# Linear attention and two gated feed-forward layers on one core: the norm's factor of tile 0 put on sums, slice groups of 3, 4 and 5, low parts by way of DRAM, decays on VectorE

## The chip, the core and the metric

The kernel runs on one core of a Trainium2 chip. A core has TensorE (matmuls out of SBUF into eight PSUM banks), VectorE, ScalarE and GpSimd for elementwise work, and queues from which DMA transfers are issued; SP's queue (SyncE) issues most of them here. The metric is the device time of one execution in microseconds. Three runs of the kernel before took 655.06, 658.07 and 658.17 us.

## What is computed

Three stages follow each other: causal linear attention with a decay for each head (in blocks of 64 in the reference, whose result doesn't depend on the block), an RMS norm with a gated layer (silu), and a second gated layer without silu.

```python
# attention, B=2, H=8, S=768, D=64, for each block of positions
intra = einsum('bhic,bhjc->bhij', qb, kb) * Dmask          # lam ** (i-j), i >= j
out[block] = einsum('bhij,bhjd->bhid', intra, vb) + einsum('bhid,bhde->bhie', qb * lam_pow, kv_state)
kv_state = lam_block * kv_state + einsum('bhsd,bhse->bhde', kb * rev_pow, vb)
...
# x: (1536, 512) tokens; first layer, d_ff = 1536
rms = sqrt(mean(x * x, axis=-1) + 1e-6);  xn = x / rms * rms_g
g = xn @ w_gate;  x = (g / (1 + exp(-g)) * (xn @ w_val)) @ w_out
# second layer
out = ((x @ w_a) * (x @ w_b)) @ w_out2
```

## The kernel before

**Tiles and slices.** The 1536 tokens are three tiles of 512 (`TILES`): tile 0 holds chunks 0 and 1 of 128 positions for both batch rows, tile 1 chunks 2 and 3, tile 2 chunks 4 and 5. The 1536 hidden features of a layer are 12 slices of 128; slices 0 to 11 are those of the first layer, 12 to 23 those of the second.

**High and low parts.** Every feed-forward product is made of three matmuls on halves: high weight with high input, high with low, low with high. ScalarE rounds a high part (`unit_hi`, word `hi` or `uh`), VectorE subtracts it from the original to get the low part (`unit_lo`, `lo` or `ul`). Both live in pools of six buffers each. Weights come in as 64-bit numbers and are first put together as 32-bit ones: two copies on ScalarE (`c`) and six operations on VectorE (`k`), for a slice's three parts together, or by pieces of 512 columns.

**Direct steps and pairs.** A direct step is one slice on one tile: a gate run G and a value run V of 12 matmuls each (`proj`), silu (`si`), product (`mu`), the two halves of it (`hh`, `hl`) and an output run O of 12 matmuls that adds into the four banks `acc0` to `acc3`. The other slices take tiles 1 and 2 together as a 2x2 block product with seven products instead of eight (`product`, word P, six matmuls each), with sums of weight blocks (`ws`) and of results (`ps`, `pa`) ahead and behind; their output runs are Q. `GROUPS` sets which slices share an accumulation: the first group of the first layer is direct on all three tiles, later groups and the whole second layer are direct on tile 0 alone and pairs on tiles 1 and 2. At a group's end `E` (or `e`) copies or adds the banks into the tile's sums (`tile_sum`).

**Attention** of a batch row b and chunk c is a handful of short TensorE groups: S (scores), X (within the chunk), I (from the state), U (state update), R (mean of squares by a column of ones) and N (the token factors, spread over the partitions by a matmul with a diagonal). VectorE masks the scores (`am`); GpSimd multiplies the keys and queries by their decays (`kd`, `qd`), decays the state (`sd`) and takes the power -1/2 (`rr`). The norm then multiplies x by g and the factor (`nx`) and splits it into tile halves (`xh`, `xl`). For chunks 2 on, VectorE first adds up the squares over the four column blocks (`rd`), so that R is one matmul and not four. W are matmuls on zeros that only keep TensorE busy.

**Order.** Nothing is scheduled: `PROGRAM` is a list of words written out by hand, run from first to last; each word issues its instructions, and each engine and each DMA queue works off its own in that order. A word `G.3` is the gate run of step 3, `X.1.0` the X of b=1, c=0, `l.6` the load of a weight part on SP's queue.

Of the kernel before, what the change touches and what calls it, by code (L numbers as in the profile page):

```python
# [38 lines left out]
GROUPS = [(0, 6), (6, 12)]  # L39

SLOTS, OUT_SLOTS = 7, 10


LAST_ATT = 11
# [4 lines left out]
    A.0.0.0 W.8.1 W.14 W.3.1 W.7.1 W.2.1 S.0.0 W.3.1 A.0.0.2 l.0 g Z A.1.0.0 A.1.0.2 D.0 D.1 A.0.1.0 A.1.1.3  # L49
    A.1.1.0 l.1 l.2 A.0.1.2 A.1.1.2 c.0.1 S.1.0 l.3 A.0.1.3 k.0.0.1 k.0.1.1 k.0.3.1 k.0.4.1 k.0.5.1 k.0.2.1  # L50
    am.0.0.0 am.0.0.1 am.1.0.0 am.1.0.1 k.0.6.1 X.0.0 kd.1.0 U.1.0 X.1.0 sq.0.0 xg.1.0 kd.0.0 S.0.1 U.0.0 hi.0.0
    xg.0.0 sa.1.0 sa.0.0 R.0.0 ms.0.0 am.0.1.0 am.0.1.1 lo.0.0 L.0.2 sq.1.0 c.0.2 S.1.1 R.1.0 k.0.0.2 am.1.1.1
    k.0.1.2 ms.1.0 c.1.0 qd.0.1 I.0.1 k.0.4.2 am.1.1.0 k.0.3.2 k.0.5.2 k.0.2.2 qd.1.1 kd.1.1 X.0.1 I.1.1 W.3.1
    sd.0.1 rr.0 dg.0 N.0 kd.0.1 W.3.1 U.1.1 W.3.1 X.1.1 U.0.1 xg.0.1 c.1.1 k.0.6.2 hi.0.1 nx.0.1 nx.0.0 xh.0.0
    sq.0.1 nx.0.2 nx.0.3 xh.0.1 xg.1.1 l.4 l.10 l.5 R.0.1 sd.1.1 lo.0.1 xl.0.0 sa.1.1 sa.0.1 ms.0.1 xl.0.1 sq.1.1
    R.1.1 ms.1.1 c.1.2 k.1.0 L.1.2 k.1.1 c.2.0 qd.0.2 kd.0.2 rr.1 dg.1 k.1.4 k.1.3 N.1 nx.1.3 nx.1.2 nx.1.0 nx.1.1
# [812 lines left out]
```

## Time and profile before

| | |
|---|---|
| three runs | 655.06, 658.07, 658.17 us (median 658.07) |
| profiled execution | 655.5 us, its span 653.8 us |
| TensorE busy | 638.9 us, 98% |
| VectorE busy | 520.1 us, 80% |
| ScalarE busy | 405.0 us, 62% |
| GpSimd busy | 39.7 us, 6% |

The span runs from the first to the last instruction of the profiled execution; 1.7 us lie around it. Busy times of engines overlap each other. A TensorE group's own duration includes its pipeline's drain, so consecutive groups overlap by a little.

### The profile page before, as it was taken

The page shows a single profiled execution, that of the slowest core. Times are in us where ns is not written, and L with a number is a line of the kernel's source. Part 1 is how long each engine was busy: PE and PEld are TensorE (multiplying, and loading weights), DVE is VectorE, ACT ScalarE, POOL GpSimd, SP SyncE. Part 2 cuts the span into 40 slices and gives each one's busy share as a digit, 9 for nine tenths or more (in the row PEclk, how much of TensorE's full clock was granted, in tenths as well). Part 3 has the DMA queues.
Part 4 walks back from the last instruction along what each step waited for, and adds up shares of the span by engine and source line. Part 5 has one row for each costly group of instructions (what it writes and reads, how often), then busy time and mean ns, then how long its engine had stood idle before and what let it go on. Part 6 is the DMA issues. An engine that isn't in the chain of part 4 may idle for free.

```text
span 653.8 us, 8719 instructions
## 1 busy us (share of the span) xinstructions
PE 638.9 (98%) x3304; PEld 517.5 (79%) x3306; DVE 520.1 (80%) x889; ACT 405.0 (62%) x642; POOL 39.7 (6%) x43
## 2 busy tenths in 40 slices
PE   9989999999999999999999999999999999999997
PEld 4767777787888888878887888888887888888876
DVE  4789999655579999889999988857968688776664
ACT  2878853332599884379888655665559873444441
POOL 1533122110000000000000000000000000000000
PEclk9969999999999999999999999999999999999999
DMA  8945641110036520013233120020023220100011
GB/s 262 378 156 188 226 161 65 65 65 1 4 127 194 162 96 1 1 36 126 66 99 127 64 65 1 0 66 33 1 96 97 67 63 1 65 1 0 2 64 65
DMA packets 16506, 54.84 MB, mean 84 GB/s; under 512 B 1864, under 2 KB 3408, under 8 KB 15440
## 3 DMA queue, kind: packets, MB, share of 16 engines
q1 hardware_dynamic: 15600, 47.99, 22.2%
q10 hardware_dynamic: 864, 6.29, 2.7%
q8 instruction: 26, 0.43, 0.3%
q14 instruction: 16, 0.13, 0.1%
HBM read 51.12 MB, written 3.15 MB: 83 GB/s over the span
## 4 chain that ended last, share of the span: by engine, by line
PE 86%; DVE 9%; DMA 2%; SPq 1%; ACT 1%; issue 0%; POOL 0%; ACTq 0%; DVEq 0%; POOLq 0%
PE acc L562 27%; PE at L706 15%; PE gv L706 11%; PE gv L514 6%; PE gv L518 6%; PE gv L515 5%; PE at L515 3%; PE at L514 3%; PE at L518 3%; DMA att<-att_dram 1%; DVE sums L574 1%; PE at L393 1%; PE at L358 1%; DVE wlo L317 1%; PE at L408 1%; DVE hh L301 1%
## 5 line engine op out<-in xcount | busy, mean ns | idle before, releaser
L260 ACT COPY hh<-stage 128x1024 uint8<-128x1024 uint8 x72 | 75.2, 1045 | 6.7 <-DMA stage<-w_dram 6.5
L514 PE MATMUL gv<-xhi,whi 128*128 128x512 f32 x192 | 76.7, 399 | 0.0
L317 DVE TENSOR_TENSOR wlo<-w,whi 128x512 fp32r<-128x512 f32 (+1 forms) x108 | 69.7, 654 | 7.8 <-ACT whi L312 7.8
L515 PE MATMUL gv<-xlo,whi 128*128 128x512 f32 x192 | 74.9, 390 | 0.0
L312 ACT CAST whi<-w 128x512 fp32r<-128x512 f32 (+1 forms) x108 | 60.5, 585 | 14.1 <-PE acc L562 5.6
L537 ACT CAST hhi<-s 128x512 fp32r<-128x512 f32 x36 | 22.4, 622 | 50.7 <-DVE s L533 49.1
L317 DVE TENSOR_TENSOR wlo<-o,whi 128x512 fp32r<-128x512 f32 x72 | 50.5, 705 | 3.5 <-ACT whi L312 3.4
L518 PE MATMUL gv<-xhi,wlo 128*128 128x512 f32 x192 | 51.6, 391 | 1.4 <-DVE wlo L317 1.4
L264 ACT COPY w<-stage 128x1024 uint16<-128x1024 uint16 x48 | 50.2, 1045 | 0.0
L312 ACT CAST whi<-o 128x512 fp32r<-128x512 f32 x72 | 44.2, 620 | 8.9 <-PE acc L562 4.3
L518 PEld LDWEIGHTS gv<-xhi,wlo 128*128 128x128 f32 x192 | 35.9, 188 | 9.7 <-DVE wlo L317 2.2
L562 PE MATMUL acc<-hlo,whi 128*128 128x512 f32 x144 | 42.1, 392 | 0.9 <-DVE hlo L541 0.6
L562 PE MATMUL acc<-whi,hlo 128*128 128x512 f32 x144 | 42.9, 391 | 0.0
L514 PEld LDWEIGHTS gv<-xhi,whi 128*128 128x128 f32 x192 | 36.1, 188 | 8.4 <-issue 0.9
L562 PE MATMUL acc<-hhi,whi 128*128 128x512 f32 x144 | 42.5, 395 | 0.2
L562 PE MATMUL acc<-whi,hhi 128*128 128x512 f32 x144 | 42.2, 392 | 0.1
L562 PE MATMUL acc<-wlo,hhi 128*128 128x512 f32 x144 | 41.8, 390 | 0.0
L515 PEld LDWEIGHTS gv<-xlo,whi 128*128 128x128 f32 x192 | 36.1, 188 | 7.0
L562 PE MATMUL acc<-hhi,wlo 128*128 128x512 f32 x144 | 41.5, 390 | 0.0
L706 PE MATMUL at<-T,whi 128*128 128x512 f32 x144 | 38.5, 389 | 0.0
L514 PE MATMUL at<-xhi,whi 128*128 128x512 f32 x96 | 37.3, 389 | 0.0
L515 PE MATMUL at<-xlo,whi 128*128 128x512 f32 x96 | 37.3, 389 | 0.0
(167 smaller groups left out, 1405.0 us busy)
## 6 DMA issues: line engine op xcount, KB each, us to landing
stage<-w_dram SPq DMA_DIRECT2D x72, 512.0 KB, 3.4
att<-att_dram ACTq DMA_DIRECT2D x6, 1024.0 KB, 4.8
att<-att_dram SPq DMA_DIRECT2D x6, 512.0 KB, 5.6
out_dram<-sums SPq DMA_DIRECT2D x12, 256.0 KB, 2.1
att<-att_dram SPq DMA_DIRECT2D x2, 1024.0 KB, 8.3
att<-att_dram SPq DMA_DIRECT2D x4, 256.0 KB, 9.6
dt<-ext_d SPq DMA_DIRECT2D x2, 256.0 KB, 4.7
p<-ext_d SPq DMA_DIRECT2D x2, 128.0 KB, 4.6
```

Of the source, the lines that this page charges most:

```text
L260: nc.scalar.copy(hh_t[i][:, into].bitcast(U8).rearrange("p (n e) -> p n e", e=2), st.rearrange("p (n e) -> p n e", e=8)[:, :, 3:5],)
L264: nc.scalar.copy(home(i, slice(place, place + 1)).bitcast(U16).rearrange("p (n e) -> p n e", e=2), st.bitcast(U16).rearrange("p (n e) -> p ...
L301: nc.vector.tensor_tensor(out=hh, in0=hh, in1=t, op=ALU.bitwise_or)
L312: nc.scalar.copy(whi[key], src)
L317: nc.vector.tensor_sub(wlo[key], src, whi[key].bitcast(F32))
L358: nc.tensor.matmul(ps[r][:, a * C : (a + 1) * C], lhsT=t[r * D : (r + 1) * D, 1, a * C : (a + 1) * C], rhs=t[r * D : (r + 1) * D, 0, a * C ...
L514: nc.tensor.matmul(ps, lhsT=w, rhs=xhi[t][:, k, :], start=k == 0, stop=False)
L515: nc.tensor.matmul(ps, lhsT=w, rhs=xlo[t][:, k, :], start=False, stop=False)
L518: nc.tensor.matmul(ps, lhsT=w, rhs=xhi[t][:, k, :], start=False, stop=k == KD - 1)
L537: nc.scalar.copy(h_t[g][0], s_t[g])
L562: nc.tensor.matmul(acc[j], lhsT=lhsT, rhs=rhs, start=first and n == 0, stop=last and n == 2)
L706: nc.tensor.matmul(ps, lhsT=w[:, k * 128 : (k + 1) * 128], rhs=x[:, k, :], start=first and n == 0, stop=n == len(todo) - 1, skip_group_che ...
```

## The change

Four things change together, and with them the written-out order.

- **Norm of tile 0.** Chunks 0 and 1 go from their bank straight to tile 0's high and low halves with g alone (`xs`, `xd`). The token factors are kept in `rv`; `gs` multiplies the gate's sums by them ahead of silu, and after the last group `sr` multiplies the first layer's sums of tile 0, since the value half and the output product are linear in them. Chunks 2 to 5 are normed as before.
- **Groups.** The first layer has groups of 3, 4 and 5 slices, so 3 slices are direct on all tiles and 9 are pairs on tiles 1 and 2; the second keeps 6 and 6.
- **Low parts by way of DRAM.** The low parts of slices 0 to 2, made for tile 0, are stored (`ls`) and read back for tiles 1 and 2 (`lr`), in SP's queue: 9 stores, 18 loads of 256 KB. The high parts are rounded again.
- **Decays.** Keys and queries are multiplied on VectorE, from chunk 2 on mostly both in one instruction of 1024 columns (`qk`); the state decay moves there too. GpSimd copies the key decays once into a table (`dk`) and keeps the power. R of chunks 2 and 3 is four matmuls, as that of chunks 0 and 1; `rd` stays for chunks 4 and 5. Nine of the 46 W matmuls go, eight output buffers stay of ten.

```diff
-GROUPS = [(0, 6), (6, 12)]
...
+GROUPS = [[(0, 3), (3, 7), (7, 12)], [(0, 6), (6, 12)]]
...
+def beside(i, t):
+    return i < GROUPS[0][0][1] and t < 2 or i < GROUPS[0][1][1] and t == 0
...
-LAST_ATT = 11
...
-    A.0.0.0 W.8.1 W.14 W.3.1 W.7.1 W.2.1 S.0.0 W.3.1 A.0.0.2 l.0 g Z A.1.0.0 A.1.0.2 D.0 D.1 A.0.1.0 A.1.1.3
...
+    W.3.1 W.2.1 W.7.1 A.0.0.0 W.8.1 S.0.0 W.3.1 W.14 A.0.1.2 g l.0 A.0.0.2 Z A.1.0.0 A.1.0.2 D.0 A.0.1.0 l.1 D.1
...
+    wlo_d = dpool.tile([GROUPS[0][0][1] * 3, 128, 512], F32, tag="wlo_d", name="wlo_d")
+
+    def lo_store(g, part):
+        nc.sync.dma_start(out=wlo_d[g * 3 + part], in_=wlo[g, part].bitcast(F32))
+
+    def lo_load(g, part):
+        wlo[g, part] = spool.tile([128, 512], F32R, tag="wlo", name="wlo")
+        nc.sync.dma_start(out=wlo[g, part].bitcast(F32), in_=wlo_d[steps[g][0] * 3 + part])
...
-    def key_decay(b, c):
...
-        nc.gpsimd.tensor_tensor(
-            out=kd_t[b, c],
...
-    def query_decay(b, c):
...
+    def decay(b, c, some):
+
+        if (b, c) not in kq_t:
+            kq_t[b, c] = kq if b == 0 else spare[:, 0:1024].rearrange("p (n j) -> p n j", n=2)
+        nc.vector.tensor_tensor(
+            out=kq_t[b, c][:, some], in0=att_t[b, c][:, 0:4:3][:, some], in1=kq_dec[:, some], op=ALU.mult
+        )
+
+    def decay_table():
+
+        nc.gpsimd.tensor_copy(
+            kq_dec[:, 1].rearrange("p (a r d) -> p a r d", a=NP, r=2),
+            dt[:, :, :, C - 1 : C].rearrange("p r a o -> p a r o").to_broadcast([128, NP, 2, D]),
...
     def state_decay(b, c):
-        nc.gpsimd.tensor_tensor(
+        nc.vector.tensor_tensor(
             out=st_t[b], in0=st_t[b], in1=p1[:, :, C - 1 : C].to_broadcast([128, NP, D]), op=ALU.mult
...
+    def att_hi(b, c):
+
+        hi = xtiles(0)[0]
+        for k in range(KD):
+            nc.scalar.mul(hi[:, k, c * 256 + b * C : c * 256 + (b + 1) * C], px_t[b, c][:, k * C : (k + 1) * C], g_sb[:, k, :])
+
+    def att_lo(b, c):
+        hi, lo = xtiles(0)
+        for k in range(KD):
+            some = (slice(None), k, slice(c * 256 + b * C, c * 256 + (b + 1) * C))
+            nc.vector.scalar_tensor_tensor(
+                out=lo[some], in0=px_t[b, c][:, k * C : (k + 1) * C], scalar=g_sb[:, k, :], in1=hi[some].bitcast(F32),
+                op0=ALU.mult, op1=ALU.subtract,
+            )
...
+    def factors(c):
+        nc.scalar.copy(rv[:, c * 256 : (c + 1) * 256], pr_t[c][:, 0:256])
...
-        for m in range(2) for lo, hi in GROUPS for t in range(1 if m or lo else len(TILES)) for f in range(lo, hi)
+        for m in range(2) for lo, hi in GROUPS[m] for t in range(1 if m or lo else len(TILES)) for f in range(lo, hi)
...
+    def gate_factors(g):
+        s_t[g] = hpool.tile([128, 512], F32, tag="s", name="s")
+        nc.vector.tensor_tensor(out=s_t[g], in0=pg_t[g], in1=rv, op=ALU.mult)
...
+        i, t, _, _ = steps[g]
+        if i < NF and t == 0:
+            nc.scalar.activation(s_t[g], s_t[g], AF.Silu)
+        else:
+            s_t[g] = hpool.tile([128, 512], F32, tag="s", name="s")
+            nc.scalar.activation(s_t[g], pg_t[g], AF.Silu if i < NF else AF.Copy)
...
+    def sum_factors(j):
+        nc.vector.tensor_tensor(out=sums[0][:, j, :], in0=sums[0][:, j, :], in1=rv, op=ALU.mult)
...
```

TensorE's queue ahead of the first gate run (rows with `xhi,whi` are gate matmuls; L454 is R, L478 N, L378 U, L358 S, L393 I, L408 X; the number behind `att_2` and the like only tells buffers apart). Before:

```order
L408 MATMUL acc_348<-am,att_1_186 64x128 x8
L378 MATMUL acc_396<-att_1_184,kd 64x64 x8
L454 MATMUL acc_429<-ones,sq 128x1 x4
L454 MATMUL acc_445<-ones,sq 128x1 x4
L478 MATMUL at_472<-nrm,ones 128x128 x2
L358 MATMUL at_486<-att_2_293 128x128
...
L378 MATMUL at_509<-att_2_293,kd 64x64 x8
L393 MATMUL at_518<-qd,st 64x128 x8
L408 MATMUL at_518<-am,att_2_293 64x128 x8
L514 MATMUL gv_535<-xhi_414,whi 128x512
```

The same place after the change (L489 is R, L513 N, L398 U, L378 S, L413 I, L428 X, L552 and L553 gate or value):

```order
L428 MATMUL acc_380<-am,att_1_192 64x128 x8
L489 MATMUL acc_399<-ones,sq 128x1 x4
L398 MATMUL acc_412<-att_1_175,kq 64x64 x8
L513 MATMUL at_421<-nrm,ones 128x128 x2
L378 MATMUL at_455<-att_2_435 128x128
...
L489 MATMUL acc_465<-ones,sq 128x1 x4
L552 MATMUL gv_494<-xhi_242,whi 128x512
...
L398 MATMUL at_507<-att_2_435,kq 64x64 x8
L513 MATMUL at_516<-nrm,ones 128x128 x2
L413 MATMUL at_522<-kq,st 64x128 x8
L428 MATMUL at_522<-am,att_2_435 64x128 x8
L552 MATMUL gv_576<-xhi_242,whi 128x512
```

U, N, I and X (the last three rows and the one ahead of them) stood ahead of the first gate run and now stand behind it, and between X and the scores of chunk 2 there is one R, one U and one N.

TensorE's queue at N of chunk 3, before (L514 and L515 are the gate run of step 5, or behind N the value run):

```order
L454 MATMUL at_1103<-ones,nrm 128x1
L514 MATMUL gv_1124<-xhi_414,whi 128x512
L515 MATMUL gv_1124<-xlo_415,whi 128x512
...
L518 MATMUL gv_1124<-xhi_414,wlo 128x512 x4
L478 MATMUL at_1137<-nrm,ones 128x128 x2
L514 MATMUL gv_1145<-xhi_414,whi 128x512
```

And after (L608 is the output run of step 1):

```order
L552 MATMUL gv_910<-xhi_242,whi 128x512
...
L556 MATMUL gv_910<-xhi_242,wlo 128x512 x4
L489 MATMUL at_931<-ones,sq 128x1 x4
L513 MATMUL at_942<-nrm,ones 128x128 x2
L608 MATMUL acc_796<-hhi,whi 128x512
```

Before, a gate run lies between the last R of chunk 3 and its N; now nothing does.

GpSimd's queue for chunk 1 to 2 before (L337 keys, L349 queries, L418 state, L468 the power):

```order
L468 TENSOR_TENSOR rr<-ms,mhalf 128x2
L337 TENSOR_TENSOR kd<-att_1_184,dt 128x512
L418 TENSOR_TENSOR st<-st,p_88 128x256
L349 TENSOR_TENSOR qd<-att_2_293,p_88 128x512
L337 TENSOR_TENSOR kd<-att_2_293,dt 128x512
```

VectorE's queue at the same chunks after (L362 decays, L438 the state decay, L309 and L315 pieces of a weight's conversion, L468 `xd`, L496 epsilon):

```order
L362 TENSOR_TENSOR kq<-att_1_175,dec 128x512
L309 TENSOR_SCALAR t<-hh 128x512
...
L438 TENSOR_TENSOR st<-st,dec 128x256 x2
L468 SCALAR_TENSOR_TENSOR xlo_243<-acc_380,g_sb,xhi_242 128x128 x4
L496 TENSOR_SCALAR ms<-acc_399 128x1
L362 TENSOR_TENSOR kq<-att_2_435,dec 128x1024
```

Products that GpSimd made by itself now stand among VectorE's conversions and remainders.

## Rows read from the trace of the kernel before

**Rows 1.** the page, part 1: busy us, share of the span, instructions.

```profile
PE 638.9 (98%) x3304; PEld 517.5 (79%) x3306; DVE 520.1 (80%) x889; ACT 405.0 (62%) x642; POOL 39.7 (6%) x43
```

**Rows 2.** the page, part 4: the chain that ended last, by engine.

```profile
PE 86%; DVE 9%; DMA 2%; SPq 1%; ACT 1%; issue 0%; POOL 0%; ACTq 0%; DVEq 0%; POOLq 0%
```

**Rows 3.** busy time by stretch (columns as in its second line).

```profile
core 0: us, PE busy (x) PEld busy (x) DVE busy (x) ACT busy (x) POOL busy (x), PEclk, DMA share, GB/s
...
44.40:111.80 67.40, 63.74 (x431) 50.50 (x429) 64.27 (x106) 47.31 (x69) 16.10 (x14) 1.00 0.47 160
...
165.00:285.00 120.00, 120.00 (x534) 99.45 (x533) 102.97 (x166) 85.80 (x133) 1.00 (x1) 1.00 0.25 80
```

**Rows 4.** the chain in order of time: start us, us, what.

```profile
108.05 2.72 PE acc L562 x12
```

**Rows 5.** TensorE in order of time: start us, us, what [idle before].

```profile
14.56 1.09 PE L408 MATMUL acc<-am,att 128*64 128x128 f32 x16
15.48 0.64 PE L378 MATMUL acc<-att,spare 128*64 128x64 f32 x16
...
17.02 1.16 PE L358 MATMUL at<-att 64*128 64x128 f32 x16
...
21.82 1.09 PE L393 MATMUL acc<-qd,st 64*64 64x128 f32 x16
...
30.10 1.05 PE L454 MATMUL acc<-ones,sq 128*128 128x1 f32 x8
...
34.62 1.22 PE L478 MATMUL at<-nrm,ones 128*128 128x128 f32 x4 [1.67 <-DVE nrm L473]
...
44.40 0.50 PE L514 MATMUL gv<-xhi,whi 128*128 128x512 f32 x1
...
47.27 0.28 PE L454 MATMUL at<-ones,nrm 128*128 128x1 f32 x2
```

**Rows 6.** busy time by stretch at the start, with the granted clock (PEclk).

```profile
24.00:33.00 9.00, 8.15 (x99) 6.03 (x96) 8.24 (x19) 8.08 (x13) 5.53 (x5) 1.00 0.91 348
...
36.00:44.00 8.00, 6.40 (x60) 5.43 (x62) 7.10 (x13) 5.19 (x6) 3.67 (x3) 0.52 0.55 179
```

**Rows 7.** GpSimd in order of time.

```profile
13.31 1.06 POOL L337 TENSOR_TENSOR spare<-att,dt 128x512 f32<-128x512 f32 x1 [10.88 <-DMA dt<-ext_d]
...
52.41 1.60 POOL L349 TENSOR_TENSOR qd<-att,p 128x512 f32<-128x512 f32 x1 [7.38 <-DMA att<-att_dram]
...
102.52 1.16 POOL L337 TENSOR_TENSOR spare<-att,dt 128x512 f32<-128x512 f32 x1 [0.74 <-DMA att<-att_dram]
```

**Rows 8.** VectorE in order of time.

```profile
52.78 1.77 DVE L317 TENSOR_TENSOR wlo<-o,whi 128x512 fp32r<-128x512 f32 x1
...
104.16 2.04 DVE L301 TENSOR_TENSOR hh<-hh,t 128x1536 uint16<-128x1536 uint16 x1
```

**Rows 9.** TensorE's waits, 44.4 to 135 us: us in total, times, longest.

```profile
PE at L378 <- DVE am L369: 1.6, 2, 1.1
PE gv L518 <- DVE wlo L317: 1.4, 2, 1.2
```

**Rows 10.** VectorE's groups, forms apart: count, busy us, mean ns, idle before.

```profile
L317 DVE TENSOR_TENSOR wlo<-w,whi 128x512 fp32r<-128x512 f32 x90 | 62.1, 701 | 7.8 <-ACT whi L312 7.8
...
L428 DVE TENSOR_TENSOR st<-st,at 128x256 f32<-128x256 f32 x6 | 2.5, 414 | 0.8 <-POOL st L418 0.5 <-PE at L378 0.3
...
L301 DVE TENSOR_TENSOR hh<-hh,t 128x512 uint16<-128x512 uint16 x3 | 1.3, 425 | 0.1
...
L665 DVE TENSOR_TENSOR sums<-sums 128x1024 f32<-128x1024 f32 x1 | 1.2, 1221 | 0.0
```

**Rows 11.** DMA issues: count, KB each, median us to landing.

```profile
out_dram<-sums SPq DMA_DIRECT2D x12, 256.0 KB, 2.1
...
att<-att_dram SPq DMA_DIRECT2D x4, 256.0 KB, 9.6
```

More of the change, by code (lines that the diff above doesn't have):

```diff
@@ L199, in chain_kernel @@
     dt = cpool.tile([128, 2, NP, C], F32, tag="dt", name="dt")
-    p1 = cpool.tile([128, NP, C], F32, tag="p1", name="p1")
+    kq_dec = cpool.tile([128, 2, 512], F32, tag="dec", name="dec")
+    p1 = kq_dec[:, 0].rearrange("p (a i) -> p a i", a=NP)
+    kq = tpool.tile([128, 2, 512], F32, tag="kq", name="kq")
     g_sb = cpool.tile([128, KD, 1], F32, tag="g_sb", name="g_sb")
+    rv = cpool.tile([128, 512], F32, tag="rv", name="rv")
     ones = cpool.tile([128, 128], F32, tag="ones", name="ones")
@@ L520, in gate @@
     def gate(g):
-        pg_t[g] = bank("at0" if g > LAST_ATT and g % 2 else "gv0")
+        pg_t[g] = bank("at0" if g % 2 and not beside(*steps[g][:2]) else "gv0")
         proj(pg_t[g], g, 0)
     def value(g):
-        pv_t[g] = bank("at1" if g > LAST_ATT and g % 2 else "gv1")
+        pv_t[g] = bank("at1" if g % 2 and not beside(*steps[g][:2]) else "gv1")
         proj(pv_t[g], g, 1)
+    def gate_factors(g):
+        s_t[g] = hpool.tile([128, 512], F32, tag="s", name="s")
+        nc.vector.tensor_tensor(out=s_t[g], in0=pg_t[g], in1=rv, op=ALU.mult)
     def silu(g):
-        s_t[g] = hpool.tile([128, 512], F32, tag="s", name="s")
-        nc.scalar.activation(s_t[g], pg_t[g], AF.Silu if steps[g][0] < NF else AF.Copy)
+        i, t, _, _ = steps[g]
[4 more added lines that the diff above has]
+            nc.scalar.activation(s_t[g], pg_t[g], AF.Silu if i < NF else AF.Copy)
     def gated(g):
@@ L567, in tile_sum @@
     def tile_sum(i, t, j):
-        if i % NF == GROUPS[0][1] - 1:
+        if i % NF == GROUPS[i // NF][0][1] - 1:
             if (t, i // NF) not in sums:
@@ L716, in snapshot @@
         elif n == 6:
-            pool, tag = H2_HOMES[i % 6]
-            s_t[i, 2] = pool.tile([128, 512], F32, tag=tag, name="h2")
+            pool, tag, half = H2_HOMES[i % 6]
+            if tag not in h2_t:
+                h2_t[tag] = pool.tile([128, 1024 if tag in ("kq", "dec") else 512], F32, tag=tag, name="h2")
+            s_t[i, 2] = h2_t[tag][:, half * 512 : half * 512 + 512]
             nc.scalar.copy(s_t[i, 2], px[i])
@@ L744, in pair_out @@
         f = i % NF
-        first, last = f in [x for x, _ in GROUPS], f + 1 in [x for _, x in GROUPS]
+        first, last = (f + n in [x[n] for x in GROUPS[i // NF]] for n in range(2))
         out_part(i, (i, "u", 3 + t), h_t[i, t], first, last, slice(a, b))
@@ L778, in chain_kernel @@
         "W": keep_warm,
-        "c": conv_copy, "k": conv_op, "hi": split_hi, "lo": split_lo,
-        "kd": key_decay, "qd": query_decay, "S": scores, "am": mask, "U": key_value, "I": inter, "X": intra,
-        "sd": state_decay, "sa": state_add, "xg": att_copy,
+        "c": conv_copy, "k": conv_op, "hi": split_hi, "lo": split_lo, "ls": lo_store, "lr": lo_load,
+        "dk": decay_table, "qk": lambda b, c: decay(b, c, slice(0, 2)), "kd": lambda b, c: decay(b, c, slice(1, 2)),
+        "qd": lambda b, c: decay(b, c, slice(0, 1)), "S": scores, "am": mask, "U": key_value, "I": inter, "X": intra,
+        "sd": state_decay, "sa": state_add, "xg": att_copy, "xs": att_hi, "xd": att_lo,
         "sq": square, "rd": square_sum, "R": mean_square, "ms": mean_eps, "rr": rsqrt, "dg": diagonal,
-        "N": spread, "nx": norm, "xh": norm_hi, "xl": norm_lo,
-        "G": gate, "V": value, "si": silu, "mu": gated, "hh": gated_hi, "hl": gated_lo, "O": out_proj,
-        "E": group_sum,
+        "N": spread, "rv": factors, "nx": norm, "xh": norm_hi, "xl": norm_lo,
+        "G": gate, "V": value, "gs": gate_factors, "si": silu, "mu": gated, "hh": gated_hi, "hl": gated_lo, "O": out_proj,
+        "E": group_sum, "sr": sum_factors,
         "bh": between_hi, "bl": between_lo, "th": block_hi, "tl": block_lo, "td": block_diff,
```

273 lines of the change are left out of this document (133 added, 140 removed).

## The prediction

> **What bounds the kernel now.** I read the page's busy table first: TensorE is busy for 638.9 of 653.8 us, VectorE for 520.1, GpSimd for 39.7 [rows 1]. The chain of work that ended last says the same of time: 86% of it runs over TensorE and 9% over VectorE [rows 2]. So a microsecond counts where it is a microsecond of matmuls, or one in which TensorE stands still. The busy times by stretch show where that is. From 165 to 285 us TensorE is busy for 120.0 of 120 us beside 103.0 us of VectorE; from 44.4 to 111.8 us it is busy for 63.7 of 67.4, and there VectorE is all but full with 64.3 [rows 3]. Before 44.40 us, where the first gate matmul of the feed-forward part starts [rows 5], TensorE does attention for two chunks and waits. The change therefore has three places: the matmul count, the start up to the first gate, and the stretch in which VectorE is full.
>
> **The matmuls.** Before, the first layer has 24 direct steps (18 for slices 0 to 5 on three tiles, 6 for slices 6 to 11 on tile 0) and 6 slices as pairs. After, it has 18 direct steps (9 for slices 0 to 2, 4 and 5 for the rest) and 9 slices as pairs. A direct step has 24 gate and value matmuls, a slice as a pair 7 products of 6, that is 42. So 6 x 24 = 144 go and 3 x 42 = 126 come: 18 fewer. The 12 output matmuls of a slice and tile are the same in both forms. Twelve full matmuls take 2.72 us of the chain [rows 4], 0.227 each: **-4.1 us**.
>
> **The start.** Before, norm stands between attention and the first gate: reciprocal root on GpSimd, a diagonal, TensorE's spread, four products, two roundings, two remainders. After, chunks 0 and 1 go from their bank to tile 0's halves (g alone), and the token factor comes later, on the gate's sums and on the layer's sums. What then stands before the first gate is TensorE's own queue. The masks need the decay table, which lands when GpSimd's first product starts, at 13.31 us [rows 7]; three masks of 0.6 us later, at 15.4, the first X can start. Up to the gate the order has 4 X, 3 S, 4 U, 2 I, 4 R and one N. By their rows [rows 5] that is 4 x 1.09 + 3 x 1.16 + 4 x 0.64 + 2 x 1.09 + 4 x 1.05 + 0.7 = 17.5 us (N at 0.7, since its row is at the lower clock, where everything there takes nearly twice as long). One wait is certain: S.0.2 needs the bank that `rv.0` copies, 0.5 us. The gate starts near 15.4 + 17.5 + 0.5 = 33.4 us, 11.0 earlier. Not all is won: U.0.2, N.1, I.0.2 and X.0.2 now follow G.0, at full clock 0.64 + 0.7 + 1.09 + 1.09 = 3.5 us. Net **-7.5 us**. From below, the groups overlap by some 0.07 us each, so 32 us is possible (-9); from above, an arrival of chunk 1 late by 2 us gives -5.5.
>
> **What the change adds to TensorE's path.** R of chunks 2 and 3 no longer gets squares that VectorE has summed: four matmuls of one column for one, 1.05 us for 0.28 [rows 5], four times 0.77: **+3.1 us**, and four of VectorE's reduces go for it. R.1.3 and N.3 now stand side by side in TensorE's queue. Between them lie epsilon (VectorE), the root (GpSimd) and the diagonal (VectorE); the same chain ahead of N.1 before made TensorE wait 1.67 us [rows 5]. Nothing else is queued between: **+1.7 us**; O.1 and S.0.4 behind it are late by as much. It would be nothing if VectorE were already that late, so 0 to 1.7.
>
> **VectorE.** It takes over 14 products for the decays (6 of 128x1024 at 1.22, 8 of 128x512 at 0.70 us) and 8 state decays at 0.41 [rows 10]: 16 us; 12 gate products with the factor, 4 on the sums and 12 more group additions at 0.70: 20 us; and 3 slices more as pairs. It loses the low parts that now come back from DRAM, the reduces and half of norm. Summed over all forms that is near +25 us, 545 us of 646: under TensorE still, and most of it lies after 165 us beside a full TensorE [rows 3]. In the first stretch the balance is better than before: only three slices must be converted before tile 1 starts, not six. Two points are tight, the low parts of V.0 and of G.1: from the last `xd` VectorE has a wide decay, two masks, the state additions and 14 conversion pieces of at most 0.42 us ahead of the first of them [rows 10], some 9 us, while TensorE has 6.2 us (G.0 and the 3.5 us above) and 1.8 us of V.0's own high part. I take **+1.0 us** (0 to 4).
>
> GpSimd's products leave. Beside one of 1.60 us, a split that takes 0.70 on average took 1.77; beside the one at 102.52 us an OR took 2.04 [rows 7, 8, 10]. Behind them TensorE waited 1.1 us for a mask and 1.2 us for a low part, the longest of their groups [rows 9]. With no product on GpSimd these go: **-2.3 us**. The Trainium skill (SBUF — State Buffer, "SBUF: two separate sides") says that GpSimd and a VectorE instruction with two SBUF inputs exclude each other for whole instructions; the durations above agree. Taken at full worth, it would free VectorE of nearly all of GpSimd's time in that stretch, and all 3.7 us of TensorE's idle time there would go [rows 3], 1.4 us more than I count.
>
> **The low parts by way of DRAM.** Nine stores and 18 loads of 256 KB go through SP's queue, between the weights. Such a transfer took 2.1 us on an idle ring (the output) and 9.6 us in the crowded start [rows 11]. In the order the loads of tile 1 stand at least two runs of twelve matmuls, over 5 us, ahead of their use, those of tile 2 about four. The store's own cover is the step that uses the low part. I take nothing, with a price below.
>
> **Sum**, on the profiled span: 653.8 - 4.1 - 7.5 + 3.1 + 1.7 + 1.0 - 2.3 = 645.7 us; with the 1.7 us around the span, 647.4, against 655.5 for that execution. The median shown is 658.07, 2.6 us over the profiled one, the lowest 655.06. I write 648.
>
> **Rivals.**
> - *The clock.* At 33 us the granted clock fell to half: the stretch from 36 to 44 us shows 0.52 after 1.00 from 24 to 33 [rows 6]. Ahead of that TensorE had done products of one column and waited. The change takes out nine dense filler matmuls at 25 to 28 us, and the same thin products stand right before G.0. If ten microseconds at half clock fall on the first gates, each dense microsecond costs one more, up to 5 us: 653. For it: the fall itself. Against it: shorter waits than before. The Trainium skill (TensorE: Matmul & The Clock Gate, "Part 1") calls the low clock the default that only activity lifts, which speaks against taking filler out; the fall at 33 us agrees.
> - *More than I count.* Start at 32 us, no wait at N.3, and all of the 3.7 us: 648 - 1.5 - 1.7 - 1.4 - 1 = 642 to 643.
> - *The start isn't earlier.* If S.0.2 waits for chunk 2, or VectorE delivers the last `xd` only near 40 us, then -7.5 becomes about -1: 654 to 655, no change to measure. Against it: VectorE's work from 13.3 us to that point is 8 masks and 6 decays at 0.6 to 0.7, 8 conversion pieces, 16 quarter operations on `xd` (the trace has 128x256 at 0.41 [rows 10], so 0.2 to 0.4 each) and little else, 15 to 19 us, so 32 at the latest.
> - *The reloads are late (slower).* Each load holds SP's queue until its slot is free, and the weights behind it wait. The gain of 8.1 us and the 3.3 us of the measurement are used up when the 18 reloads delay TensorE by 0.63 us each. At the crowded landing time of 9.6 us against a lead of 5 to 9 us, an exposed 0.6 to 1 us each gives 659 to 666. Against it: the rings are 0.47 full in the crowded stretch after the gate and 0.25 later [rows 3].
>
> **How the numbers follow.** 0.5% of this kernel is 3.3 us, and less than that a measurement can't tell from no change. Forecast 0.55 (own range 644 to 652), clock 0.17 (650 to 656), more 0.12 (639 to 644), start not earlier 0.08 (653 to 656), reloads 0.08 (659 to 666). Against 658.1 less 3.3, faster means under 654.8: all of the forecast and of "more", half of the clock, a quarter of "not earlier": 0.77, which I take down to 0.75 for what I haven't seen. Same: 0.15. Slower: 0.10. The range that leaves out less than 2 in 10: 640 to 657.
>
> **What would show it.** In the profile after, the first gate matmul at 32 to 35 us; R groups of 1.05 us for chunks 2 and 3; a wait of TensorE for VectorE's diagonal ahead of N.3; no VectorE instruction drawn out beside GpSimd; reload landings of 2 to 5 us, and no TensorE wait named after `wlo_d`. I'm wrong if the granted clock is at half beyond the first gate, if the first gate starts at 40 us, or if TensorE's idle time from the gate to 165 us exceeds 4 us.

## The result, and the profile after

The changed kernel took 646.8 us (median of four runs, 644.74 to 647.85) against 657.8 us for the kernel before on the same chip: ratio 0.9841, with an interval from 0.9817 to 0.9864. The profiled execution took 646.6 us, its span 644.9 us. The forecast was 648.0, the working's sum 645.7 us for the span. How that number came about is another matter: the start and the rest are each off by 5 us or more, with opposite signs.

The page of the kernel after, its busy table and the chain that ended last [rows 1, 2]:

```profile
PE 633.8 (98%) x3303; PEld 517.4 (80%) x3303; DVE 538.8 (84%) x966; ACT 416.0 (65%) x664; POOL 5.9 (1%) x16
...
PE 93%; DMA 2%; DVE 2%; ACT 1%; SPq 1%; issue 0%; POOL 0%; ACTq 0%; POOLq 0%
```

TensorE is busy for 5.1 us less, VectorE for 18.7 us more, and VectorE's part of the chain has gone from 9% to 2%. Before, TensorE stood idle for 14.9 us of the span, now for 11.1.

TensorE in order of time after the change, from the R of chunk 0, b=1, up to the second run of the feed-forward part, `V.0`, which starts at 44.81 us [rows 5] (L489 is R, L413 I, L428 X, L398 U, L513 N, L378 S, L552 and L556 gate or value):

```profile
15.70 1.96 PE L428 MATMUL acc<-am,att 128*64 128x128 f32 x30 [1.01 <-DVE am L389]
...
21.28 1.16 PE L378 MATMUL gv<-att 64*128 64x128 f32 x16 [0.40 <-DMA att<-att_dram]
22.37 1.49 PE L489 MATMUL acc<-ones,sq 128*128 128x1 f32 x8
23.79 1.97 PE L413 MATMUL acc<-kq,st 64*64 64x128 f32 x16
25.69 1.97 PE L428 MATMUL acc<-am,att 128*64 128x128 f32 x16
27.45 1.07 PE L398 MATMUL acc<-att,spare 128*64 128x64 f32 x16
28.45 1.65 PE L413 MATMUL acc<-spare,st 64*64 64x128 f32 x16
30.03 1.09 PE L428 MATMUL acc<-am,att 128*64 128x128 f32 x16
...
35.53 1.05 PE L489 MATMUL acc<-ones,sq 128*128 128x1 f32 x8 [0.43 <-ACT sq L475]
36.45 0.77 PE L552 MATMUL gv<-xhi,whi 128*128 128x512 f32 x1
...
39.96 1.09 PE L556 MATMUL gv<-xhi,wlo 128*128 128x512 f32 x4
40.98 0.69 PE L398 MATMUL at<-att,kq 128*64 128x64 f32 x16
41.59 0.71 PE L513 MATMUL at<-nrm,ones 128*128 128x128 f32 x4
42.77 1.09 PE L413 MATMUL at<-kq,st 64*64 64x128 f32 x16 [0.46 <-ACT rv L518]
43.79 1.09 PE L428 MATMUL at<-am,att 128*64 128x128 f32 x16
44.81 0.50 PE L552 MATMUL gv<-xhi,whi 128*128 128x512 f32 x1
```

The same gate run's low-part rows and the start of `V.0` in the kernel before (L518 is the low part, L514 `V.0`):

```profile
46.35 1.08 PE L518 MATMUL gv<-xhi,wlo 128*128 128x512 f32 x4
...
47.41 0.48 PE L514 MATMUL gv<-xhi,whi 128*128 128x512 f32 x1
```

The first gate starts at 36.45 us, 7.95 us earlier than before [rows 5]. But five attention rows from 22 to 30 us take 1.4 to 1.8 times as long as the same rows elsewhere, and the first eight gate matmuls are drawn out too. Busy time by stretch after the change, with the granted clock as the third figure from the end [rows 3, 6]: two stretches at half clock (1.2 of 2.4 GHz), 10.2 us together and so as long as the one before the change (33.4 to 43.6 us), and the whole rest from `V.0` on at full.

```profile
22.80:29.60 6.80, 6.80 (x66) 6.34 (x67) 4.01 (x12) 1.14 (x4) 0.71 (x1) 0.50 0.81 328
36.50:39.90 3.40, 3.40 (x9) 2.72 (x10) 3.40 (x12) 2.75 (x3) 0.69 (x1) 0.50 0.94 353
44.80:644.90 600.10, 592.93 (x2928) 487.63 (x2926) 508.12 (x878) 394.46 (x625) 2.90 (x4) 1.00 0.25 83
```

The same for the kernel before:

```profile
33.40:43.60 10.20, 7.38 (x56) 6.18 (x58) 9.02 (x19) 7.41 (x9) 4.12 (x4) 0.50 0.56 181
47.41:653.80 606.39, 597.40 (x2921) 487.79 (x2919) 489.10 (x819) 376.98 (x603) 21.13 (x19) 1.00 0.21 69
```

All of TensorE's waits from the first gate to 165 us in the kernel after (us in total, times, longest) [rows 9], and the two new groups of DMA issues [rows 11]:

```profile
PE at L513 <- DVE nrm L508: 1.4, 1, 1.4
PE at L489 <- DVE am L389: 0.8, 1, 0.8
PE at L513 <- ACT sq L475: 0.7, 1, 0.7
PE at L413 <- DVE ms L496: 0.5, 2, 0.3
PE at L413 <- ACT rv L518: 0.5, 1, 0.5
```

```profile
wlo<-wlo_d SPq DMA_DIRECT2D x18, 256.0 KB, 2.7
...
wlo_d<-wlo SPq DMA_DIRECT2D x9, 256.0 KB, 3.8
```

The waits add up to 3.9 us; none is for a weight or its low part. A reload lands 2.7 us after its issue in the median.

### The profile page after: what moved, and what is told of

It reads as the page before. It is cut to its first block, busy times and chain, and to the rows that moved or that the text cites. A ratio compares the mean times of both kernels' runs of the same rounds, so it can differ in the third digit from the quotient of the medians.

```text
span 644.9 us, 8832 instructions
## 1 busy us (share of the span) xinstructions
PE 633.8 (98%) x3303; PEld 517.4 (80%) x3303; DVE 538.8 (84%) x966; ACT 416.0 (65%) x664; POOL 5.9 (1%) x16
## 4 chain that ended last, share of the span: by engine, by line
PE 93%; DMA 2%; DVE 2%; ACT 1%; SPq 1%; issue 0%; POOL 0%; ACTq 0%; POOLq 0%
PE acc L608 30%; PE at L755 18%; PE gv L755 13%; PE gv L552 6%; PE gv L553 6%; PE gv L556 6%; PE at L552 3%; PE at L556 3%; PE at L553 3%; PE at L413 1%; PE at L378 1%; DMA att<-att_dram 1%; PE at L428 1%; DVE sums L620 1%; DMA ext_d<-nrm 1%; PE at L398 0%
## 5 line engine op out<-in xcount | busy, mean ns | idle before, releaser
L552 PE MATMUL gv<-xhi,whi 128*128 128x512 f32 x160 | 65.2, 407 | 0.0
L553 PE MATMUL gv<-xlo,whi 128*128 128x512 f32 x160 | 63.3, 396 | 0.0
L333 DVE TENSOR_TENSOR wlo<-w,whi 128x512 fp32r<-128x512 f32 (+1 forms) x90 | 55.4, 624 | 8.9 <-ACT whi L328 8.6
L755 PE MATMUL at<-T,whi 128*128 128x512 f32 x172 | 46.0, 389 | 0.0
L608 PE MATMUL acc<-hhi,whi 128*128 128x512 f32 x144 | 44.0, 396 | 0.1
L608 PE MATMUL acc<-hlo,whi 128*128 128x512 f32 x144 | 43.9, 389 | 0.0
L608 PE MATMUL acc<-whi,hlo 128*128 128x512 f32 x144 | 43.0, 389 | 0.0
L608 PE MATMUL acc<-hhi,wlo 128*128 128x512 f32 x144 | 43.0, 390 | 0.0
L556 PE MATMUL gv<-xhi,wlo 128*128 128x512 f32 x160 | 42.8, 389 | 0.0
L608 PE MATMUL acc<-whi,hhi 128*128 128x512 f32 x144 | 41.7, 390 | 0.0
L608 PE MATMUL acc<-wlo,hhi 128*128 128x512 f32 x144 | 41.5, 389 | 0.0
L333 DVE TENSOR_TENSOR wlo<-wsum,whi 128x512 fp32r<-128x512 f32 x42 | 28.9, 688 | 13.0 <-ACT whi L328 12.9
L755 PEld LDWEIGHTS at<-T,whi 128*128 128x128 f32 x172 | 32.3, 188 | 6.7
L552 PEld LDWEIGHTS gv<-xhi,whi 128*128 128x128 f32 x160 | 30.5, 191 | 7.8 <-issue 1.0
L772 ACT COPY usum<-at 128x512 f32<-128x512 f32 x32 | 18.7, 586 | 27.6 <-PE at L755 27.4
L553 PEld LDWEIGHTS gv<-xlo,whi 128*128 128x128 f32 x160 | 30.6, 192 | 6.0
L556 PEld LDWEIGHTS gv<-xhi,wlo 128*128 128x128 f32 x160 | 30.2, 189 | 6.4
```

The source lines that it names most:

```text
L333: nc.vector.tensor_sub(wlo[key], src, whi[key].bitcast(F32))
L552: nc.tensor.matmul(ps, lhsT=w, rhs=xhi[t][:, k, :], start=k == 0, stop=False)
L553: nc.tensor.matmul(ps, lhsT=w, rhs=xlo[t][:, k, :], start=False, stop=False)
L556: nc.tensor.matmul(ps, lhsT=w, rhs=xhi[t][:, k, :], start=False, stop=k == KD - 1)
L608: nc.tensor.matmul(acc[j], lhsT=lhsT, rhs=rhs, start=first and n == 0, stop=last and n == 2)
L755: nc.tensor.matmul(ps, lhsT=w[:, k * 128 : (k + 1) * 128], rhs=x[:, k, :], start=first and n == 0, stop=n == len(todo) - 1, skip_group_che ...
```

## The experiments

Each kernel was timed beside the kernel before; its medians in those sets were 656.4 to 656.7 us. The changed kernel was timed in the first set alone, beside the kernel before at 657.8 us, so a difference of medians to it is uncertain by about 1 us; the ratios allow for that. The matmuls of attention that lie ahead of `V.0` are the same in all kernels but for one R, so the time of `V.0` cuts each profile in two: the start, and what is left to the span's end. Times in us; the last three columns are those of one profiled execution each, and the start's length differs by some us between executions of one kernel, by how long the clock is low in it.

| kernel | median | ratio to before, interval | first gate | `V.0` | `V.0` to the end |
|---|---|---|---|---|---|
| before | 657.8 | 1 | 44.40 | 47.41 | 606.4 |
| after | 646.8 | 0.9841, 0.9817 to 0.9864 | 36.45 | 44.81 | 600.1 |
| norm of tile 0 back | 658.9 | 1.0051, 1.0030 to 1.0071 | 50.24 | 53.46 | 603.7 |
| norm back, 26 fillers | 656.4 | 1.0003, 0.9979 to 1.0028 | 46.72 | 49.57 | 603.6 |
| decays back on GpSimd | 652.0 | 0.9932, 0.9909 to 0.9956 | 35.82 | 44.17 | 605.1 |
| before, decays on VectorE | 662.2 | 1.0086, 1.0067 to 1.0105 | 50.18 | 53.17 | 607.2 |
| low parts made again | 659.1 | 1.0051, 1.0029 to 1.0072 | 38.84 | 47.39 | 613.7 |
| the same, the first one later | 652.5 | 0.9943, 0.9922 to 0.9963 | 38.33 | 46.67 | 605.7 |
| the same with 13 fillers | 651.0 | 0.9907, 0.9882 to 0.9932 | 35.23 | 42.02 | 607.2 |
| 13 fillers | 644.1 | 0.9814, 0.9794 to 0.9834 | 34.24 | 41.01 | 600.2 |
| N.3 later | 647.2 | 0.9855, 0.9819 to 0.9890 | 36.22 | 44.58 | 600.5 |
| squares on VectorE | 649.1 | 0.9887, 0.9849 to 0.9925 | 38.89 | 47.21 | 600.4 |
| fillers, N.3, squares | 644.3 | 0.9820, 0.9803 to 0.9838 | 34.93 | 41.72 | 600.9 |
| before, 15 fillers | 655.5 | 0.9982, 0.9964 to 1.0000 | 46.97 | 50.00 | 606.3 |

**Norm of tile 0 back in its old place,** all else as after the change:

```diff
-    U.0.2 N.1 rv.1 ... X.0.2        (behind G.0)
+    U.0.2 N.1 nx.1.0 nx.1.1 nx.1.2 nx.1.3 xh.1.0 xh.1.1 xl.1.0 xl.1.1 ... X.0.2 G.0
-    xs.0.0 xd.0.0 ... gs.0 ... sr.0
+    xg.0.0 ...
```

> The changed kernel with the norm of tile 0 back in its old place: chunks 0 and 1 are copied, multiplied by the factor and split, the first gate run stands behind the attention of chunk 2 of the first batch row again, and the products with the factor on gate and sums are gone. Theory of the prediction (the earlier first gate is the largest part of the gain): the first gate starts at 42 to 45 us instead of 36.5, and the time is 4 to 7 us over the changed kernel's 646.8, about 651 to 654. Rival (VectorE's lighter load after the gate is the gain, and the start is made good later): at most 2 us over it.

658.9 us, 12.1 more than after the change and past both expectations. TensorE in order of time in this kernel, at S and I of chunk 2 (L376, L411):

```profile
35.48 2.05 PE L376 MATMUL at<-att 64*128 64x128 f32 x14 [3.13 <-DVE xg L520]
...
46.44 1.97 PE L411 MATMUL at<-kq,st 64*64 64x128 f32 x16 [3.90 <-DVE spare L520]
```

Two waits for norm's products, and from 33.9 to 51.0 us the clock is at half. To tell waits from clock, the same kernel got fillers (W, matmuls on zeros) where it waits; the order has 26, not the 28 of the expectation:

```diff
-    N.0 ... S.0.2 R.1.1 ... N.1 ... I.0.2
+    N.0 W.7.1 ... S.0.2 W.2.1 R.1.1 ... N.1 W.8.1 ... I.0.2
```

> The changed kernel with tile 0's norm back between attention and the first gate, as in the run with that edit alone, and with 28 filler matmuls in the start, 15 of them in the two places where TensorE waits for norm's products (3.13 and 3.90 us), so that the granted clock should stay at full. Compared with the fillers alone (644.07 us). Theory A (the earlier start is worth the waits for norm itself, as the prediction's -7.5 us has it; the rest of the 12 us was clock): 651 to 653 us. Theory B (the whole 12 us are waits, clock beside the point): 655 to 657 us.

656.4 us, 12.3 more than with fillers alone: theory B's time. The clock is mended only in part (at half still from 37.7 to 44.5 us), but `V.0` stands 8.6 us behind that of the kernel with fillers alone, and without fillers on both sides it is 8.65. TensorE in order of time at I of chunk 2 in the kernel with 26 fillers:

```profile
44.67 1.09 PE L411 MATMUL at<-kq,st 64*64 64x128 f32 x16 [0.49 <-DVE spare L520]
```

Behind eight fillers it still waits for norm's product, so that product and not the clock sets the time; U and N ahead of it, at half clock, are about 1 us longer than at full. So of the 12 us, 8.6 are the start, most of it norm's chain, and 3.5 come later. Those I did not count at all. TensorE in the first of the two kernels, at the gate run of step 3:

```profile
81.19 0.51 PE L550 MATMUL gv<-xhi,whi 128*128 128x512 f32 x1 [2.10 <-ACT s L570]
```

It waits for ScalarE's silu to empty a bank; 3.4 us at half clock follow (81.7 to 85.1 us, some 1.7 us lost). Together that is 3.8 us.

**The decays back on GpSimd:**

```diff
     def decay(b, c, some):
-        nc.vector.tensor_tensor(
+        nc.gpsimd.tensor_tensor(
...
     def state_decay(b, c):
-        nc.vector.tensor_tensor(
+        nc.gpsimd.tensor_tensor(
```

> The changed kernel with the decays of keys, queries and state on GpSimd again, at the same places of the order. Theory (GpSimd's products hold up VectorE's instructions, and TensorE waited 2.3 us for that before): VectorE's instructions beside a GpSimd product are drawn out to 1.2 us and more, and the time is 1 to 4 us longer, 648 to 651. Rival (VectorE's load is what counts, and 14 us leave it): 0 to 2 us shorter than 646.8.

652.0 us, 5.2 more, all of it behind `V.0` (605.1 for 600.1). VectorE, GpSimd and TensorE in order of time at the norm of chunk 3 in this kernel:

```profile
81.51 2.54 DVE L508 TENSOR_SCALAR nrm<-ident,rr 128x128 f32<-128x128 f32 x2 [0.87 <-POOL rr L503]
```

```profile
81.43 2.34 POOL L362 TENSOR_TENSOR kq<-att,dec 128x1024 f32<-128x1024 f32 x1
```

```profile
83.91 1.23 PE L513 MATMUL at<-nrm,ones 128*128 128x128 f32 x4 [3.47 <-DVE nrm L508]
```

And the same row of VectorE in the kernel after:

```profile
80.84 0.48 DVE L508 TENSOR_SCALAR nrm<-ident,rr 128x128 f32<-128x128 f32 x2 [0.87 <-POOL rr L503]
```

Two diagonals take 2.54 us beside GpSimd's product of 2.34 us; in the kernel after, with GpSimd idle, 0.48 us. They end at 84.05, after GpSimd's instruction at 83.77. N.3 waits 3.47 us for 1.41, and the clock is at half for 3.4 us behind that wait. Idle time from `V.0` to 105 us is 6.4 us for 3.4, and with the clock's 1.7 us this accounts for 4.7 of the 5.0. The rival fails in its premise: 16 us of products leave VectorE, but its busy time falls only from 538.8 to 537.5 us, as its other instructions are drawn out.

**Only the decays on VectorE, in the kernel before:**

```diff
     def key_decay(b, c):
-        nc.gpsimd.tensor_tensor(
+        nc.vector.tensor_tensor(
```

and likewise in `query_decay` and `state_decay`.

> The kernel before with one part of the change alone: the decays are VectorE's products, with separate instructions for keys and queries, at their old places. Contention theory alone (what counts is that GpSimd's products no longer hold up VectorE): 1 to 3 us shorter than the kernel before. Load theory (VectorE is full from 44 to 112 us there, 64.3 of 67.4 us, and gets some 9 us of products in it for 5 us of drawn-out time that goes): 1 to 4 us longer.

662.2 us, 5.6 more than before. `V.0` starts 5.8 us later, the rest is 0.8 us longer. TensorE waits in the start:

```profile
25.00 1.09 PE L393 MATMUL acc<-qd,st 64*64 64x128 f32 x16 [1.64 <-DVE qd L349]
...
39.95 1.23 PE L478 MATMUL at<-nrm,ones 128*128 128x128 f32 x4 [2.71 <-DVE nrm L473]
```

With 1.55 us more for a decayed key at 16.97 us, and 2.71 for 1.67 at N.1, these waits are 4.2 of the 5.8 us; the clock is at half for 13.6 us of this start, for 10.2 before. Behind `V.0` the wait for a low part falls from 1.4 to 0.6 us, that for masks only from 1.6 to 1.4, and there are new ones of 1.0 us for the summed squares and 0.6 for the state. So the contention that I priced at 2.3 us is real where an instruction meets it, but taking it away gains nothing by itself: VectorE is late by as much for its new load.

**The low parts made again by VectorE,** without DRAM:

```diff
-    ls.0.0 ... lr.3.0 ... lr.3.1         (9 stores, 18 loads)
+    hi.3.0 lo.3.0 V.0 ... lo.3.1         (18 lo, each where the load stood or right behind its hi)
```

> The changed kernel with no way by DRAM: the 18 low parts of slices 0 to 2 for tiles 1 and 2 are subtracted again on VectorE, at the place of the load or right behind the rounded high part. VectorE gets 18 x 0.6 = 10.8 us more. Theory of the prediction (TensorE sets the pace, the loads are worth little): within 2 us of 646.8, 646 to 649, since VectorE is busy for 25.3 of 30 us from 75 to 105 us and has room after. Rival (VectorE is the tight engine up to 165 us): 4 to 10 us longer, with TensorE waiting for low parts.

659.1 us, 12.3 more. Here VectorE and TensorE in order of time at 50 us:

```profile
54.56 0.69 DVE L331 TENSOR_TENSOR wlo<-w,whi 128x512 fp32r<-128x512 f32 x1 [5.38 <-ACT whi L326]
55.17 0.68 DVE L387 TENSOR_TENSOR am<-at,dt 128x512 f32<-128x512 f32 x1
```

```profile
55.91 1.46 PE L487 MATMUL at<-ones,sq 128*128 128x1 f32 x8 [4.39 <-DVE am L387]
```

VectorE isn't full there, it stands still: the low part `lo.3.0` waits 5.38 us for ScalarE's high part, the masks behind it in the queue are late, and TensorE waits 4.39 us for one. That is a price of the place, not of the work; 6.8 us at half clock follow, from 56 us on. With that one word 30 steps later:

```diff
-    hi.3.0 lo.3.0 V.0 l.10 S.1.2 ... sq.1.2 lo.3.1
+    hi.3.0 V.0 l.10 S.1.2 ... sq.1.2 lo.3.0 lo.3.1
```

> The changed kernel with the eighteen low parts made again by VectorE, as in the run without the way over DRAM, but the very first of them no longer right behind its high part: it stands beside the second one, some 40 steps of the order later. In that run VectorE's queue stood still for 5.38 us at this low part, because ScalarE delivered the high part only at 54.56 us, and TensorE stood for 4.39 us behind a mask queued after it. Theory A (place in the queue): most of the 12 us were this one wait and the low clock after it; 647 to 650 us. Theory B (VectorE's load: 18 x 0.69 = 12.4 us more of VectorE in the stretch in which it is nearly full): 654 to 659 us.

652.5 us: 6.6 of the 12.3 us were the place, and 5.7 stay. And with the fillers in the start:

> The low parts on VectorE, placed as in the first run of this set, with the 13 fillers in the start. Theory A (place in the queue): at most 2 us over the fillers with the way over DRAM (644.07), 644 to 646. Theory B (VectorE's load): 650 to 656.

651.0 us, 6.9 more than with fillers and the way over DRAM. Behind `V.0` the low parts cost 5.6 and 7.0 us. Part of it shows as waits that the kernel after doesn't have; TensorE in order of time, in the last kernel (L487 is R of chunk 4, L753 a product):

```profile
112.90 0.35 PE L487 MATMUL at<-ones,nrm 128*128 128x1 f32 x2 [1.42 <-DVE nrm L477]
...
196.60 0.50 PE L753 MATMUL at<-xhi,whi 128*128 128x512 f32 x1 [1.61 <-ACT usum L770]
```

In both, VectorE delivers late, once directly and once by way of ScalarE. They are 3.0 us, and the kernel with the later low part has them too, at 116 and 200 us. In the one with fillers a stretch at half clock from 48.2 to 51.6 us loses some 1.7 us more. The rest, 2.3 to 2.6 us, I could not place.

**Fillers in the start.** Thirteen matmuls on zeros more, in five places up to the S of chunk 2:

```diff
-    S.1.0 ... R.0.0 ... I.1.1 ... N.0 ... S.0.2
+    S.1.0 W.4 ... R.0.0 W.3.1 ... I.1.1 W.2.1 ... N.0 W.2.1 ... S.0.2 W.2.1
```

> The changed kernel with 13 filler matmuls more at the start: four behind the scores of chunk 0, three behind the first mean of squares, two each behind the second I of chunk 1, the first spread and the scores of chunk 2. Clock theory (the two stretches at half clock, 22.8 to 29.6 and 36.5 to 39.9 us, come from thin TensorE work and cost 3.2 and 1.6 us): the granted clock stays whole up to the first gate, that starts at 33 to 35.5 us, and the time is 2 to 4 us under 646.8. Rival (the falls come anyway, or the start is set by arrivals and by ScalarE): the same time, or up to 2 us more for the fillers.

644.1 us, the lowest of all. Busy time by stretch in this kernel, the start and from `V.0` on:

```profile
20.00:41.00 21.00, 20.26 (x233) 15.86 (x232) 18.49 (x55) 13.94 (x26) 1.40 (x2) 1.00 0.79 297
41.00:641.20 600.20, 593.00 (x2928) 487.64 (x2926) 508.68 (x879) 394.40 (x625) 2.89 (x4) 1.00 0.25 83
```

The clock is at full throughout, the first gate starts at 34.24 us in spite of 13 matmuls more, `V.0` 3.8 us earlier, and everything behind it takes 600.2 us for 600.1. The medians differ by 2.7 us; by the ratios to the kernel before it is 1.8 us, and their intervals overlap. So the size is uncertain, but the rows show where it lies: in the start.

The same in the kernel before, behind the R and N of chunks 0 and 1, S.0.2 and U.0.2:

```diff
-    R.0.1 R.1.1 ... N.1 ... S.0.2 ... U.0.2
+    R.0.1 W.3.1 R.1.1 W.3.1 ... N.1 W.3.1 ... S.0.2 W.3.1 ... U.0.2 W.3.1
```

> The kernel before with five times three filler matmuls, three each behind the R of chunk 0 and of chunk 1, N.1, S.0.2 and U.0.2, where the granted clock was at half from 33.4 to 43.6 us. Theory A (the low clock is a price of its own): the half-clock stretch goes; of its 10.2 us some 5.5 were busy with rows that take twice as long, less 3.4 us of fillers, half of them inside waits of 0.75, 1.67 and 1.11 us: 1 to 3 us faster than before, 654 to 656. Theory B: the waits set that stretch's end, not the clock; within 1 us of before, or slower by the fillers.

655.5 us, 1.2 less, with an interval that reaches to no change. In the profile the clock is at half from about 22 to 25 and from 38 to 45 us, 10.2 us as without fillers. (Of the 10.2 us in the kernel before TensorE is busy for 7.4, not for the expectation's 5.5.) But this execution, 658.0 us, is one of the slowest of the twelve. The three with a mean granted clock of 0.999 or 1.0 took 653.3 to 654.6 us; the 29 of the kernel before beside them never show more than 0.992, and those at 0.992 took 655.1 to 657.1. The medians of the two groups are 654.2 and 655.8 us. So a start at full clock is worth some 1.6 us there, fillers included, and these fillers bring it only in some executions.

**N.3 behind the next output run:**

```diff
-    R.1.3 ms.1.3 rr.3 dg.3 mu.2 N.3 nx.3.3 k.3.4 O.1
+    R.1.3 ms.1.3 rr.3 dg.3 mu.2 k.3.4 O.1 N.3 nx.3.3
```

> The changed kernel with the spread N of chunk 3 behind the output run of step 1 instead of ahead of it. Theory (TensorE's wait of 1.41 us at N of chunk 3 is lost time): that wait goes and the time is 1.0 to 1.7 us shorter, about 645.3. Rival (the time is taken back by the next wait, for the scores of chunk 4 whose banks the norm of chunk 3 still reads): the same within 0.5 us.

647.2 us, no change. The wait of 1.41 us ahead of N.3 is gone; TensorE in order of time shows the one that takes its place, at S of chunk 4:

```profile
84.75 1.13 PE L376 MATMUL at<-att 64*128 64x128 f32 x14 [1.42 <-DVE spare L520]
```

S needs the bank that norm's products read. The chain from R.1.3 over epsilon, root, diagonal and products sets that time, at both places of N.3.

**The squares of chunks 2 and 3 summed by VectorE again** (`rd` behind `sq.0.2`, `sq.1.2`, `sq.0.3`, `sq.1.3`):

> The changed kernel with the squares of chunks 2 and 3 added up on VectorE again, so that the mean is one matmul and not four. Theory (the four longer means cost TensorE 4 x 0.77 = 3.1 us): 1.5 to 3 us shorter, 644 to 645.3. Rival (VectorE, busy for 22.8 of 25 us from 50 to 75 us, passes its 4 x 1.0 us on to TensorE): the same or up to 2 us longer.

649.1 us, not faster; its start happened to have more low clock (13.6 us for 10.2). Behind `V.0` it takes 600.4 us for 600.1: TensorE is busy for 2.3 us less, and the twelve matmuls saved come back as 2.6 us more of waits, for VectorE's epsilon and sums (TensorE's waits from 44 to 110 us: us in total, times, longest).

```profile
PE at L411 <- DVE ms L494: 1.6, 2, 0.8
...
PE at L487 <- DVE nrm L477: 0.8, 1, 0.8
PE at L376 <- DVE ms L494: 0.8, 1, 0.8
```

**Fillers, N.3 later and squares together:**

> The changed kernel with the last three edits together: fillers, the spread of chunk 3 later, squares added up on VectorE. If each is worth what its own theory says, and they don't take from each other: 5 to 8 us under 646.8, 639 to 642. If they share one cover (VectorE is late in any case): 1 to 3 us under it.

644.3 us: the fillers' gain alone.

## Why the prediction came out right, point by point

**The time is right because two errors cancel.** By my terms `V.0` should have started at 33.4 + 2.85 (a gate run) + 3.5 = 39.8 us, 7.6 earlier than before. It started at 44.81, 2.6 earlier. From `V.0` on my other terms gave -4.1 + 3.1 + 1.7 + 1.0 - 2.3 = -0.6 us; the profile shows 600.1 for 606.4, -6.3. So the start fell short by 5.0 us and the rest beat its sum by 5.7. That the total fits is luck.

**The start (-7.5 us; got -2.6).** The step that failed is taking every row of the start at full clock. I had the fall of the clock as a rival at 0.17, with the first gates as its place. It came there (36.5 to 39.9 us, 1.56 us lost on the gate run: 3.51 us to the low-part rows for 1.95 before) and also from 22.8 to 29.6 us, where five rows lost 3.2 us; sum 4.8, which is the rival's price of up to 5 us; its 653 us did not come, because the rest gained 5.7 more. Fillers took both stretches away and moved `V.0` to 41.01, 1.2 us from my 39.8. Of the signs that I named, the first gate came later than 32 to 35 us, and the clause on what would prove me wrong, half clock beyond the first gate, holds by the letter: eight of the gate run's twelve matmuls are at half. TensorE's idle time from the gate to 165 us, 3.9 us, stays just under my 4. The Trainium skill (TensorE: Matmul & The Clock Gate, "Part 1") calls the low clock the default that activity lifts; that thirteen fillers lifted it in the whole start agrees. Norm put back costs more than the term: 8.6 us of start and 3.5 us later, by the two runs with norm back. That is no measure of what moving it brought: their `V.0` at 49.57 and 53.46 us is later than the 47.41 of the kernel before, whose order was written for norm there. The later part is a wait for silu and the clock behind it, and no term of mine had it.

**The low parts by way of DRAM (nothing).** That reloads would not be late was right: 2.7 us to land, no wait for one. What failed is the other half of the step: I booked the 18 low parts as VectorE's load only and gave them no price on the path. With them made again, and the one that held up the queue moved, the kernel takes 5.7 to 6.9 us more; 2.3 to 2.6 us of that are not placed.

**GpSimd's contention (-2.3).** Undone in the kernel after it costs 5.2 us; done alone in the kernel before it gains nothing (-2.3 expected of the mechanism, +5.6 measured in all). So the term has no fixed size. My reading of the rows was wrong in part: of the two waits that I put down to GpSimd, the one for a mask is still 0.9 us without its products (1.1 before). That the gain needs VectorE's load taken off in the same stretch fits both runs, but no run shows it. The Trainium skill (SBUF — State Buffer, "SBUF: two separate sides") says that GpSimd and a VectorE instruction in a two-port mode, or with two SBUF inputs, exclude each other for whole instructions; 2.54 us for a row of 0.48, ending just after GpSimd's product, agrees. The diagonal has one tensor as input, so it would fall under the first kind; no row names an instruction's mode.

**N.3 (+1.7; measured 1.41)** was right in size, and the chain that I named is what TensorE waits for; its reason, the place of N.3, is not: with O.1 between R.1.3 and N.3 the same 1.4 us stand at S of chunk 4. **R of chunks 2 and 3 (+3.1):** the rows are there (1.05 us), but giving the squares back gains nothing: 2.3 us less of TensorE's work bring 2.6 us more of waits, so the net cost is about 0, and the term left out what VectorE gains. **The matmuls (-4.1):** behind `V.0` the trace has 2454 matmuls of 128x512 for 2472, the 18 fewer of the prediction, 4.1 us by 0.227; no run isolates it. **VectorE's two tight points (+1.0):** no wait for a low part in the kernel after; the waits for a mask and for epsilon that there are, 0.79 and 0.5 us, make 1.3. VectorE's load grew by 18.7 us, not by 25.

What the 6.3 us behind `V.0` consist of: idle time of TensorE fell from 9.0 to 7.2 us, its busy time from 597.4 to 592.9. With 18 matmuls at 4.1 us and R's rows in the sum, TensorE's busy time is 3.5 us lower than I can put to an edit. Counted from start to start, the 128x512 matmuls behind `V.0` take about 7 us less, 3 more than 18 of them are worth: they start late by over 0.09 us in some 50 places before and in some 36 after. What makes them late there is open. Undone one by one, norm, decays and low parts cost 3.5 + 5.0 + 5.6 = 14.1 us there, more than twice what all bring together. A likely reason is that the order is written for the set: each undo pays for its own work and for standing in an order that has no room for it. No run shows that, and the regrouping was not undone alone, so how the 6.3 us divide among the edits stays open.

## What to carry to other kernels

Cut the profile at an instruction that all versions share, and compare a forecast with both sides of it: a total that agrees can hide two errors. An edit undone in an order made for the whole change can measure more than the edit brings, and done alone in the old order less; before believing such a price, look whether one misplaced word in an in-order queue makes it. Where a change empties the thin stretch ahead of dense work, look at the granted clock there first; here a few fillers were worth more than moving N.3 or the squares, which brought nothing.

## What the runs showed of the hardware that was not expected

In the kernel after, the clock fell at 22.8 us, behind waits of 1.01 and 0.40 us and products of one column, and stayed at half for 6.8 us in which TensorE was busy without a gap; rows of 1.09 us took 1.97. Thirteen matmuls more, of 128x512 in bfloat16, made the kernel 2.7 us faster in the median (1.8 by the ratios). And the same start doesn't run the same way twice: the kernel with the squares has the same program ahead of the first gate as the changed kernel, and reached that gate at 38.89 us for 36.45, with 13.6 us at half clock for 10.2. Its runs spread from 644.45 to 653.89 us; those of the kernel with fillers alone, whose profile shows no low clock, from 642.9 to 645.36. A full clock came without fillers too: of the six runs of the kernel with N.3 later, one had a mean granted clock of 0.999 and took 642.4 us, the others 0.988 to 0.996 and 645.1 to 650.9 us. So the fillers make the full clock frequent; the time they give is the clock's.
